# VectorE's order at attention's end, and map loads on SyncE, in a fused attention and mixture-of-experts kernel

## The chip, the cores and the metric

The kernel runs on one core of a Trainium2 chip. The metric is the device time of one execution in microseconds (us). TensorE (PE) does the multiplications and, as PEld, loads their weights; VectorE (DVE) and ScalarE (ACT) work on tiles; GpSimd (POOL) issues gathers, scatters and small transfers; SyncE (SP) issues the large loads.

## The reference

```
scores = scale * q @ k^T ; scores = cap * tanh(scores / cap)      # B=8, H=12, S=448, D=64
attn   = exp(scores - max) / (sum + 1e-9) ; x = attn @ v          # x: 3584 tokens x 768
logits = x @ w_gate + modality_bias[modality] ; e = argmax        # 8 experts
gate   = softmax(logits)[e]
out    = gate * (relu(x @ w1[e]) @ w2[e])                         # w1: 768x1024, w2: 1024x768
```

Every token goes to one expert, so the second half gathers the tokens of one expert and multiplies them with that expert's weights.

## The kernel before, in words

**Attention.** A quad is four heads of one batch; there are NQ = 24, numbered 0 to 23, three per batch. The loop at L748 runs over 25 rounds `i` of three parts `r`. Each part lists its work in order (`ORDER` L714; `LAST` L726 for the round after the last quad). `group` makes scores, tanh and exp; `pv` and `pvs` multiply with v into two PSUM accumulators; `xs` copies an accumulator to SBUF; `tot1`, `tot2` (L590 to L600) add the three key blocks of a half quad on VectorE; `sums` (L606) multiplies with the gate's weights and sums up the denominators on TensorE; `gl` copies that from PSUM; `lt` turns it by transposition; `den` (L638) takes reciprocals and scales the logits (7 small VectorE instructions); `rows` (L662) turns x by blocks of 32 on VectorE and stores it to the DRAM table `xd` by GpSimd. The route of a batch (L227) finds each token's expert and its rank there, and scatters a map of tokens to DRAM (`mapd`).

**Early rows.** The expert with the most tokens is known before the last batches are done. Its first 384 rows are gathered (L788) while attention still runs, and its w1 is loaded and split ahead. Three steps make the first multiplication's input of them. `scale` (L680) multiplies the gathered rows with the reciprocal denominators: twelve VectorE instructions, six for each half of the 768 columns, over both halves at once. `turn_rows(half, banks)` (L992) transposes nine 128x128 blocks on TensorE into three PSUM banks. `split_x` (L1045) makes of each bank a rounded copy (ScalarE, L1048) and a remainder (VectorE, L1050), because every product is a sum of three: high by high, high by low, low by high. The six banks are three tiles of two banks each, so that the third bank of the first half and the first of the second half belong to one tile; the last bank is also where `lt` of quad 22 goes, which `den` of quad 22 reads. `hi_part` and `lo_part` (L690, L694) split w1 in halves of a chunk, on ScalarE and VectorE.

**Slots.** A slot is 384 rows of one expert. `run_slot` (L1112) does `ffn1` (L1052; eight passes `f` of 18 multiplications) and `ffn2` (L1083; 144 multiplications, cut into six stretches `2*t + half` of eight places `f`). Around them stand the next slot's loads and splits. In the first slot the routing of the last batch, the counts and the plan of slots (`slots`, L331) stand between the passes of `ffn1`; the next slot's rows are then gathered, scaled and turned at places of `ffn2` that the table at L1129 to L1134 names. In later slots the rows are turned on VectorE instead (`prepare`, L1030). `ahead` (L1234) issues for slot i its gather, then `rows` (L860: reads the slot's first row into a register, then loads the map, five small transfers for a slot of 384 rows) and `index` (L888, GpSimd) for slot i + 1, then `expert` (L857: SyncE reads the expert's number into a register). The w1 and w2 loads of all slots go through SyncE in program order (L98), into four buffers `raw`.

**Order.** Instructions wrapped in `pin` keep their place behind the instruction written before them on their engine; the others may be placed by the program's scheduler. Around the change nearly all are pinned.

Of the kernel before, what the change touches and what calls it, by code (L numbers as in the profile page):

```python
# [61 lines left out]
TW = W // 128  # L62
RB = -(-NT // W)
RG = RB * W
NOROW = E * RG
KC, FC = DM // 128, FF // 128
# [3 lines left out]
FIXED = 7  # L70
# [14 lines left out]
class Program:  # L85
# [365 lines left out]
    def attention(self, first, rp):  # L451
        tc, nc = self.tc, self.nc
        pe, pin = nc.tensor, self.pin
        with ExitStack() as st:
# [143 lines left out]
            def tot2(q, t):  # L598
                tot = quads[q]["tot"][t]
                pin(nc.vector.tensor_tensor(tot, tot, quads[q]["pt"][t, 2], op=ALU.add))  # L600
# [79 lines left out]
            def scale(q):  # L680
                three = pp.tile([128, KU, 2, S], F32, name="pt", bufs=3).rearrange("p n j s -> p (n j s)")
                banks.extend(tile[:, j] for tile in (score_tile(), score_tile(), score_tile()) for j in range(2))
                self.scale_rows(early[1], [three[:, i * 384 : (i + 1) * 384] for i in range(2 * TW)])

            def part(n):
                k, cs = n if n < KC else (n + 4) % KC, slice(n // KC * 512, n // KC * 512 + 512)
# [15 lines left out]
            def load_parts(*ns):  # L702
# [23 lines left out]
            LAST = (  # L726
                ((pvs, -1), (xs, -1, 0)),
                ((pv, -1, 1, 0), (pv, -1, 1, 1), (pv, -1, 1, 2), (xs, -1, 1)),
                ((sums, -1), (gl, -1), (rows, -1, 0), (rows, -1, 1)),
            )  # L730
            PICK, KNOWN = 2, 6
            PARTS = [PICK * NH + u for u in (6, 7, 9, 10, 12, 13, 15, 16)]
# [3 lines left out]
                *((NQ - 1, r) for r in (0, 0, 1, 1, 1)),  # L736
                *((b * NH + 5 + u, r) for b in range(B - 2) for u, r in ((0, 0), (0, 2), (0, 2), (0, 2), (1, 1), (1, 2))),
            ]
            lgs, pays, routing, raws, banks = {}, {}, [], [], []
            fetch(0, 0)  # L740
            fetch(0, 1)
            begin()
# [5 lines left out]
            for i in range(NQ + 1):  # L748
                for r in (1, 0, 2) if i == 0 else range(3):
                    if (i, r) == (0, 1):  # L750
                        split_hi(0, 1)
                        split_lo(0, 1)
                    if (i, r) == (NQ, 0):
                        tot1(NQ - 1, 1)
                        tot2(NQ - 1, 1)
                    ops = list((ORDER if i < NQ else LAST)[r])
                    if (i, r) == (NQ - 1, 2):
                        ops[-4:] = (scale, 0), (lt, -1), ops[-2]
                    if (i, r) == (NQ - 1, 1):
                        ops.insert(ops.index((sums, -1)), (lambda q: next(routing[0]), 0))  # L760
                    for op, n, *how in ops:
                        q = i + n
                        if 0 <= q and quads[min(q, NQ)]["live"]:
                            op(q, *how)
                    if r == 1:
                        fetch(i + 2, 0)
                    if r == 2:
                        fetch(i + 2, 1)
                        fetch_v(i + 2)
                    for _ in range(STEPS.count((i, r))):  # L770
                        next(routing[0], None)
                    if (i, r) in WAYS:
                        way(WAYS[i, r])
                    if (i, r) == (0, 2):
                        room = self.lp.tile([128, C * 256], F32, name="room", tag="late", bufs=3)[:CP]
                        self.gate_bias(room[:, : B * C * E].rearrange("p (n e) -> p n e", e=E), room[:, B * C * E : B * C * (E + 1)])
                    if (i, r) == (0, 0):
                        pin(nc.vector.memset(self.xg, 0.0))
                    if r == 1 and 1 <= i <= 4:
                        self.empty_map(5 * (i - 1), 5 * i)  # L780
                    if (i, r) == (PICK * NH + 4, 1):
                        chosen = self.early_expert(self.cpool, self.ps_r)
                        next(chosen)
                        meta = next(chosen)
                        e = self.expert(meta, 0)
                    if (i, r) == (KNOWN * NH + 4, 0):
                        early = e, self.rows(meta, 0)[0]
                        self.gather_rows(early[1], known=KNOWN * S)  # L788
                    if (i, r) == (KNOWN * NH + 4, 1):
                        self.early_full(self.ps_r)  # L790
                    if r == 1 and i in PARTS:
                        hi_part(PARTS.index(i))
                    if r == 1 and i + 1 in PARTS:
                        load_parts(PARTS.index(i + 1))
                    if (i, r) == (NQ - 1, 2):
                        self.make_x()
                        for n in range(KEPT, 2 * KC, 2):
                            load_parts(n, n + 1)
                    if (i, r) == (NQ, 0):
                        self.turn_rows(0, banks[:3])  # L800
                        self.split_x(range(3), banks[:3], pin=pin)
                        den(NQ - 2)
                    if (i, r) == (NQ, 1):
                        self.turn_rows(1, banks[3:])
                        self.split_x(range(3, KC), banks[3:], pin=pin)
                        rows(NQ - 2, 0)
                        rows(NQ - 2, 1)
                        hi_part(KEPT)
                        hi_part(KEPT + 1)
                        lo_part(KEPT)  # L810
                    if (i, r) == (NQ, 2):
                        hi_part(KEPT + 2)
                        lo_part(KEPT + 1)
                        hi_part(KEPT + 3)
                        lo_part(KEPT + 2)
                        lo_part(KEPT + 3)
# [40 lines left out]
    def expert(self, meta, row):  # L857
        return self.register(self.nc.sync, meta[row : row + 1, 0:1], E - 1, self.last_sp)

    def rows(self, meta, row, blocks=None):  # L860

        nc = self.nc
        r = self.register(nc.gpsimd, meta[row : row + 1, 1:2], NOROW)
        mt = self.lp.tile([128, TW, MR], F32, name="mt", bufs=6)
        src = self.mapd[ds(r, W)]
        if blocks is None:
            self.pin(nc.gpsimd.dma_start(mt.rearrange("p t w -> p (t w)"), src.rearrange("(p t) w -> p (t w)", t=TW)))
            return mt, None, None
        raw = self.lp.tile([128, 4 * TW, MR], F32, name="map", bufs=2)
        for t, n in blocks:  # L870
            rows = src[t * 128 : (t + n) * 128]
            for a in range(4):
                if n:
                    part = rows.rearrange("(p x) w -> p (x w)", p=32)
                    at = raw[a * 32 : (a + 1) * 32, 4 * t : 4 * (t + n)].rearrange("p x w -> p (x w)")
                else:
                    part = src[:128].rearrange("(g p) w -> p g w", g=4)
                    at = raw[a * 32 : (a + 1) * 32, :4]
                self.pin(nc.gpsimd.dma_start(at, part))
            if n:  # L880
                part = rows.rearrange("(p g t) w -> g p (t w)", p=32, g=4)
                at = mt[:, t : t + n].rearrange("p t w -> p (t w)")
            else:
                part, at = src[:128], mt[:, 0]
            self.pin(nc.gpsimd.dma_start(at, part))
        return mt, raw, blocks

    def index(self, raw, blocks, name="at"):  # L888
# [79 lines left out]
            raw = raws[k] if k < len(raws) else self.load_raw(e, self.w2, k, DM)  # L968
            self.split_w(raw, self.w2s[k], pin=bool(raws))

    def scale_rows(self, mt, homes):

        for i, xn in enumerate(homes):
            half, t = divmod(i, TW)
            for j in range(2):
                rec = mt[:, t, 2 + j * KC + half * 3 : 2 + j * KC + half * 3 + 3]
                self.pin(self.nc.vector.tensor_tensor(
                    xn.rearrange("p (k j d x) -> p j k d x", k=3, j=2, d=2)[:, j],
                    self.xg[:, 4 * t + 2 * j : 4 * t + 2 * j + 2, half * 96 : (half + 1) * 96].rearrange(
                        "p d (k x) -> p k d x", k=3  # L980
                    ),
                    rec.unsqueeze(2).unsqueeze(3).to_broadcast([128, 3, 2, 32]),
                    op=ALU.mult,
                ))
        self.scaled = homes
# [126 lines left out]
    def run_slot(self, cur, n, ahead=None, between=()):  # L1112
# [14 lines left out]
        if nxt and nxt[2]:  # L1127
            if between:
                at = {  # L1129
                    place: lambda k=k: self.load_w1(nxt[0], (k,))  # L1130
                    for k, place in enumerate(((0, 2), (0, 6), (1, 2), (1, 6), (2, 2), (2, 7)))
                }
                at[2, 4] = lambda: self.scale_rows(nxt[1], self.homes())
                at[3, 4], at[4, 2] = lambda: self.transpose_rows(0), lambda: self.transpose_rows(1)  # L1134
            else:
                at = self.prepare(nxt[0], nxt[2], 2 * n)
        elif nxt:
# [91 lines left out]
    def run_slots(self, cur, order):  # L1229
# [4 lines left out]
        def ahead(i, n=TW):  # L1234
# [6 lines left out]
            else:  # L1241
                self.gather(indices[i], 4 * n or 1)
            for s in [i + 1] if i < FIXED else range(i + 1, FIXED + 3) if i == FIXED else ():
                maps.append(self.rows(meta, s, BLOCKS[s]))
                indices[s] = self.index(*maps[s][1:], name="at" if s <= FIXED else f"at{s}")
            if i == FIXED:
                few.append(self.rows_few(meta, FIXED + 2))
# [246 lines left out]
```

## Time and profile before

| | |
|---|---|
| median of 3 runs | 810.02 us (808.63 to 810.65) |
| the profiled execution, of its own | 808.62 us |
| its span in the profile | 806.9 us |
| PE busy | 792.1 us (98%) |
| DVE / ACT / POOL busy | 555.8 / 513.7 / 307.1 us |
| HBM traffic | 173 GB/s over the span |

The span runs from the first to the last instruction; the 1.7 us between it and the execution's own time lie outside. PE's busy time counts matmuls whose ends are modelled, and pipelined ones overlap, so 98% says that PE has little idle time, not that it runs at its peak. The profile also has the clock that TensorE was granted, as a share of 2.4 GHz: 0.50 is 1.2 GHz.

### The profile page before, as it was taken

The page shows a single profiled execution, that of the slowest core. Times are in us where ns is not written, and L with a number is a line of the kernel's source. Part 1 is how long each engine was busy: PE and PEld are TensorE (multiplying, and loading weights), DVE is VectorE, ACT ScalarE, POOL GpSimd, SP SyncE. Part 2 cuts the span into 40 slices and gives each one's busy share as a digit, 9 for nine tenths or more (in the row PEclk, how much of TensorE's full clock was granted, in tenths as well). Part 3 has the DMA queues.
Part 4 walks back from the last instruction along what each step waited for, and adds up shares of the span by engine and source line. Part 5 has one row for each costly group of instructions (what it writes and reads, how often), then busy time and mean ns, then how long its engine had stood idle before and what let it go on. Part 6 is the DMA issues. An engine that isn't in the chain of part 4 may idle for free. (4 is left out here: it accounts for less than half of the span.)

```text
span 806.9 us, 14580 instructions
## 1 busy us (share of the span) xinstructions
PE 792.1 (98%) x5265; PEld 623.4 (77%) x5265; DVE 555.8 (69%) x1082; ACT 513.7 (64%) x597; POOL 307.1 (38%) x376
## 2 busy tenths in 40 slices
PE   7999999999999998999999999999999999999996
PEld 3444454444454444999999999999999999999995
DVE  7889898999999998967274653747537375356820
ACT  7999999999999996345253452534525354245611
POOL 1121423242324155438655173551745417015201
PEclk9999999999999999999999999999999999999998
DMA  6475564646546543576367373563725627247663
GB/s 212 143 238 186 152 191 126 208 155 188 186 150 198 160 157 128 166 279 208 118 199 238 114 229 117 180 235 113 258 100 171 243 98 241 100 146 264 214 240 132
DMA packets 55945, 144.84 MB, mean 180 GB/s; under 512 B 11567, under 2 KB 19585, under 8 KB 55858
## 3 DMA queue, kind: packets, MB, share of 16 engines
q1 hardware_dynamic: 40960, 109.42, 40.3%
q0 software_dynamic: 14752, 34.33, 13.8%
q8 instruction: 46, 0.75, 0.4%
q14 instruction: 41, 0.34, 0.1%
q10 hardware_dynamic: 146, 0.00, 0.0%
HBM read 114.91 MB, written 24.34 MB: 173 GB/s over the span
## 5 line engine op out<-in xcount | busy, mean ns | idle before, releaser
L1067 PE MATMUL ph<-x,ah 128*128 128x384 f32 (+1 forms) x480 | 156.3, 326 | 0.9 <-issue 0.9
L1068 PE MATMUL ph<-x,ah 128*128 128x384 f32 (+1 forms) x480 | 156.0, 325 | 0.0
L1071 PE MATMUL ph<-x,al 128*128 128x384 f32 (+1 forms) x480 | 156.0, 325 | 0.0
L1101 PE MATMUL py<-bh,hh 128*128 128x384 f32 x448 | 150.3, 336 | 0.0
L1101 PE MATMUL py<-bh,hl 128*128 128x384 f32 x448 | 149.8, 334 | 0.0
L1101 PE MATMUL py<-bl,hh 128*128 128x384 f32 x448 | 146.5, 334 | 0.0
L534 ACT ACTIVATE pt<-sc,isc 128x896 f32<-128x896 f32 x144 | 134.8, 1010 | 5.6 <-PE sc L530 2.5
L936 POOL DMA_INDIRECT xg<-xd,at x93 | 115.0, 1237 | 48.3 <-issue 23.8
L674 POOL DMA_DIRECT2D xd<-xs x96 | 61.1, 644 | 185.0 <-DVE xs L668 179.8
L957 DVE TENSOR_TENSOR bl<-raw,bh 128x768 fp32r<-128x768 f32 x80 | 74.3, 956 | 71.3 <-ACT bh L956 58.7
L1077 ACT ACTIVATE hh<-ph 128x384 fp32r<-128x384 f32 (+1 forms) x80 | 37.6, 470 | 134.0 <-PE ph L1071 129.1
L537 ACT ACTIVATE pt<-pt,cabs 128x2688 f32<-128x2688 f32 x48 | 121.9, 2540 | 0.8
L574 PE MATMUL xT<-pt,va 128*64 128x448 f32 x576 | 118.8, 548 | 0.0
L1078 DVE SCALAR_TENSOR_TENSOR hl<-ph,hh 128x384 fp32r<-128x384 f32 (+1 forms) x80 | 42.1, 528 | 109.8 <-ACT hh L1077 109.7
L1067 PEld LDWEIGHTS ph<-x,ah 128*128 128x128 f32 x480 | 90.1, 188 | 2.6 <-ACT ah L692 1.4
L1107 POOL DMA_INDIRECT out_dram<-ot,mt x28 | 33.9, 1212 | 152.9 <-ACT ot L1106 139.3
L1071 PEld LDWEIGHTS ph<-x,al 128*128 128x128 f32 x480 | 90.1, 188 | 0.0
L1068 PEld LDWEIGHTS ph<-x,ah 128*128 128x128 f32 x480 | 90.1, 188 | 0.0
L1101 PEld LDWEIGHTS py<-bh,hh 128*128 128x128 f32 x448 | 84.1, 188 | 1.1 <-issue 0.7
L1101 PEld LDWEIGHTS py<-bh,hl 128*128 128x128 f32 x448 | 84.1, 188 | 0.0
L1101 PEld LDWEIGHTS py<-bl,hh 128*128 128x128 f32 x448 | 83.8, 188 | 0.0
L956 ACT CAST bh<-raw 128x768 fp32r<-128x768 f32 x80 | 64.0, 834 | 26.3 <-DMA raw<-in_w_dram 22.4
(213 smaller groups left out, 1298.1 us busy)
## 6 DMA issues: line engine op xcount, KB each, us to landing
raw<-in_w_dram SPq DMA_DIRECT2D x86, 384.0 KB, 4.1
raw<-in_w_dram SPq DMA_DIRECT2D x60, 512.0 KB, 5.1
kq<-in_kq_dram SPq DMA_DIRECT2D x47, 448.0 KB, 4.4
va<-in_v_dram SPq DMA_DIRECT2D x24, 448.0 KB, 6.2
xd<-xs POOLq DMA_DIRECT2D x96, 112.0 KB, 3.7
cg<-gl SPq DMA_DIRECT2D x22, 224.0 KB, 2.2
raw<-in_w_dram SPq DMA_DIRECT2D x12, 256.0 KB, 4.1
mapd<-pre SPq DMA_DIRECT2D x4, 480.0 KB, 5.6
```

The lines of the kernel that those rows point to most:

```text
L534: pin(nc.scalar.activation(out, sc[:, :, :S], AF.Tanh, scale=self.isc))
L537: pin(nc.scalar.activation(x, x, AF.Exp, scale=self.cabs))
L574: pin(pe.matmul(xT[j * D : (j + 1) * D, :S], va[:, u * D : (u + 1) * D], quads[q]["pt"][t, i][:, j], start=t == i == 0, stop=t == 1 and i ...
L674: (nc.gpsimd.dma_start(self.xd[b * S : (b + 1) * S, a, r * 64 : (r + 1) * 64].rearrange("(n p) f -> p n f", p=32), d["out"][a * 32 : (a + ...
L936: got = self.nc.gpsimd.indirect_dma_start(self.xg[:, c], None, self.xd.rearrange("n a x -> (n a) x"), bass.IndirectOffsetOnAxis(ap=at[:, c ...
L956: a = self.nc.scalar.copy(hi, raw)
L957: b = self.nc.vector.tensor_tensor(lo, raw, hi, op=ALU.subtract)
L1067: nc.tensor.matmul(ph[:, :w], hi[:, fs], self.x[k][:, 0, :w], start=first, stop=False)
L1068: nc.tensor.matmul(ph[:, :w], hi[:, fs], self.x[k][:, 1, :w], start=False, stop=False)
L1071: nc.tensor.matmul(ph[:, :w], lo[:, fs], self.x[k][:, 0, :w], start=False, stop=last)
L1078: nc.vector.scalar_tensor_tensor(hl[:, f, :w], acc, 0.0, hh[:, f, :w], op0=ALU.max, op1=ALU.subtract)
L1101: nc.tensor.matmul(py[half][:, :HALF], self.h[a][:, f, rows], self.w2s[f][c][:, cs], start=left[half] == 3 * FC - 1, stop=left[half] == 0,)
```

## The change

Three edits, all of order or place; the arithmetic is the same.

1. At attention's end. `scale` does the first half's six multiplications only; the second half's six come after the additions `tot1`, `tot2` of quad 23's second half. `den` of quad 22 moves up to directly behind its `lt`. The second half's turn and its `split_x` (`second`) move behind `sums` of quad 23. `hi_part` of two w1 parts moves ahead of it; `rows` of quad 22 and the `lo_part`s come after `rows` of quad 23.
2. In the first slot's `ffn2`, the turns of the next rows move from places (3, 4) and (4, 2) to (3, 6) and (4, 3).
3. `rows` for slots 2 to 7 (counted from 0, the third and later ones of the list `maps`; `0 < i < FIXED`, six calls) reads its register on SyncE and issues its map loads there, behind the last load that SyncE had.

```
             def scale(q):
                 three = ...
-                self.scale_rows(early[1], [three[:, i * 384 : (i + 1) * 384] for i in range(2 * TW)])
+                homes.extend(three[:, i * 384 : (i + 1) * 384] for i in range(2 * TW))
+                self.scale_rows(early[1], homes, (0,))
+
+            def second(q):
+                self.turn_rows(1, banks[3:])
+                self.split_x(range(3, KC), banks[3:], pin=pin)
             LAST = (
-                ((sums, -1), (gl, -1), (rows, -1, 0), (rows, -1, 1)),
+                ((sums, -1), (second, -1), (gl, -1), (rows, -1, 0), (rows, -1, 1)),
             )
                     if (i, r) == (NQ, 0):
                         tot1(NQ - 1, 1)
                         tot2(NQ - 1, 1)
+                        self.scale_rows(early[1], homes, (1,))
                     if (i, r) == (NQ - 1, 2):
-                        ops[-4:] = (scale, 0), (lt, -1), ops[-2]
+                        ops[-4:] = (scale, 0), (lt, -1), (den, -1), ops[-2]
                     if (i, r) == (NQ, 0):
                         self.turn_rows(0, banks[:3])
                         self.split_x(range(3), banks[:3], pin=pin)
-                        den(NQ - 2)
                     if (i, r) == (NQ, 1):
-                        self.turn_rows(1, banks[3:])
-                        self.split_x(range(3, KC), banks[3:], pin=pin)
+                        hi_part(KEPT)
+                        hi_part(KEPT + 1)
+                    if (i, r) == (NQ, 2):
                         rows(NQ - 2, 0)
                         rows(NQ - 2, 1)
-                        hi_part(KEPT)
-                        hi_part(KEPT + 1)
                         lo_part(KEPT)
-                    if (i, r) == (NQ, 2):
                         hi_part(KEPT + 2)
-    def rows(self, meta, row, blocks=None):
+    def rows(self, meta, row, blocks=None, sync=False):
-        r = self.register(nc.gpsimd, meta[row : row + 1, 1:2], NOROW)
+        if sync:
+            r = self.register(nc.sync, meta[row : row + 1, 1:2], NOROW, self.last_sp)
+            load = self.load
+        else:
+            r = self.register(nc.gpsimd, meta[row : row + 1, 1:2], NOROW)
+            load = lambda out, in_: self.pin(nc.gpsimd.dma_start(out, in_))
-                self.pin(nc.gpsimd.dma_start(at, part))      # three places, each now:
+                load(at, part)
-    def scale_rows(self, mt, homes):
+    def scale_rows(self, mt, homes, halves=(0, 1)):
         for i, xn in enumerate(homes):
             half, t = divmod(i, TW)
+            if half not in halves:
+                continue
-                at[3, 4], at[4, 2] = lambda: self.transpose_rows(0), lambda: self.transpose_rows(1)
+                at[3, 6], at[4, 3] = lambda: self.transpose_rows(0), lambda: self.transpose_rows(1)
-                maps.append(self.rows(meta, s, BLOCKS[s]))
+                maps.append(self.rows(meta, s, BLOCKS[s], 0 < i < FIXED))
```

## Rows read from the trace of the kernel before

**Rows 1.** One stage by windows: width, busy us of each engine (instructions), clock, DMA, GB/s
```profile
375.00:722.00 347.00, 347.00 (x2003) 347.00 (x2003) 187.37 (x257) 150.10 (x235) 157.95 (x173) 1.00 0.53 177
```
**Rows 2.** TensorE's timeline at attention's end: start, us, instruction, idle before it
```profile
302.74 0.58 PE L624 MATMUL glog<-tot,pick 128*32 128x448 f32 x3
...
304.00 0.54 PE L624 MATMUL glog<-sh,pick 128*32 128x448 f32 x1
...
309.53 0.65 PE L610 MATMUL sc<-ident,gl 128*112 128x128 f32 x4
...
311.02 1.20 PE L997 MATMUL sc<-ident,pt 128*128 128x128 f32 x9
312.15 2.48 PE L574 MATMUL xT<-pt,va 128*64 128x448 f32 x12
316.31 0.33 PE L997 MATMUL sc<-ident,pt 128*128 128x128 f32 x1 [1.68 <-DVE x L1050]
317.35 1.25 PE L997 MATMUL sc<-ident,pt 128*128 128x128 f32 x8 [0.71 <-DVE lg L653]
...
321.64 0.45 PE L1067 MATMUL ph<-x,ah 128*128 128x384 f32 x1
```
**Rows 3.** VectorE's timeline there
```profile
308.43 3.30 DVE L977 TENSOR_TENSOR pt<-xg,mt 128x192 f32<-128x192 f32 x12
311.64 1.09 DVE L600 TENSOR_TENSOR tot<-tot,pt 128x896 f32<-128x896 f32 x1
...
314.78 1.48 DVE L1050 TENSOR_TENSOR x<-sc,x 128x384 fp32r<-128x384 f32 x3
...
316.94 0.36 DVE L653 TENSOR_TENSOR lg<-sc,pay 112x64 f32<-112x64 f32 x2
...
319.53 1.02 DVE L1050 TENSOR_TENSOR x<-sc,x 128x384 fp32r<-128x384 f32 x2 [0.20 <-ACT x L1048]
```
**Rows 4.** ScalarE's timeline there
```profile
318.26 1.24 ACT L1048 CAST x<-sc 128x384 fp32r<-128x384 f32 x3 [3.05 <-PE sc L997]
```
**Rows 5.** The first slot's matmul line: instruction, count, ns min/median/max, first and last start
```profile
L1067 PEldq EVENT_SEMAPHORE  x1: 51/51/51, 320.6 to 320.6; - x1
```
**Rows 6.** Windows of one us (columns as in rows 1; clock third from the end)
```profile
12.00:13.00 1.00, 0.08 (x2) 0.08 (x2) 0.58 (x2) 0.97 (x2) 0.00 (x0) 1.00 1.03 419
318.00:319.00 1.00, 1.00 (x8) 0.41 (x10) 0.23 (x1) 0.74 (x2) 0.00 (x0) 0.57 0.00 0
321.00:322.00 1.00, 1.00 (x6) 0.36 (x3) 1.00 (x3) 0.58 (x2) 0.07 (x1) 0.72 0.71 163
```
**Rows 7.** Waits of TensorE: waited for, us in total, times, longest
```profile
PE sc L530 <- ACT sh L534: 2.3, 2, 1.5
```
**Rows 8.** VectorE and TensorE where the last batch's ranks are made
```profile
329.21 0.56 DVE L1078 SCALAR_TENSOR_TENSOR hl<-ph,hh 128x384 fp32r<-128x384 f32 x1 [0.99 <-ACT hh L1077]
...
331.22 0.36 DVE L255 TENSOR_TENSOR before<-before,oh 112x8 bf16<-112x8 bf16 x2
...
331.64 0.20 PE L265 MATMUL rank<-before,ones 112*112 112x32 bf16 x1
```
**Rows 9.** TensorE at the first slot's first turn
```profile
362.38 0.82 PE L997 MATMUL xt<-ident,xn 128*128 128x128 f32 x6
363.70 0.55 PE L997 MATMUL xt<-ident,xn 128*128 128x128 f32 x3 [0.50 <-DVE xn L977]
```
**Rows 10.** SyncE's issue (ns min/median/max), landing, timeline; ScalarE's use; GpSimd's wait (times)
```profile
L98 SPq DMA_DIRECT2D raw<-in_w_dram x158: 332/333/1552, 154.2 to 794.5; - x158
...
raw<-in_w_dram SPq DMA_DIRECT2D x60, 512.0 KB, 5.1
...
380.80 2.63 SPq L98 DMA_DIRECT2D raw<-in_w_dram  x3
...
401.07 1.99 ACT L956 CAST ah<-raw 128x1024 fp32r<-128x1024 f32 x2
...
  DMA out_dram<-ot,mt: 13.8, 5
```

More of the change, by code (lines that the diff above doesn't have):

```diff
@@ L738, in attention @@
             ]
-            lgs, pays, routing, raws, banks = {}, {}, [], [], []
+            lgs, pays, routing, raws, banks, homes = {}, {}, [], [], [], []
             fetch(0, 0)
@@ L866, in rows @@
         if blocks is None:
-            self.pin(nc.gpsimd.dma_start(mt.rearrange("p t w -> p (t w)"), src.rearrange("(p t) w -> p (t w)", t=TW)))
+            load(mt.rearrange("p t w -> p (t w)"), src.rearrange("(p t) w -> p (t w)", t=TW))
             return mt, None, None
@@ L884, in rows @@
                 part, at = src[:128], mt[:, 0]
-            self.pin(nc.gpsimd.dma_start(at, part))
+            load(at, part)
         return mt, raw, blocks
```

## The prediction

> **What bounds the kernel now.** I read the windows by stage first, then TensorE's waits and its timeline, because PE is busy nearly throughout. From 375 to 722 us PE has no idle time at all, while VectorE works 187 of 347 us, ScalarE 150 and GpSimd 158 [rows 1]. In these seven slots a faster helper gains nothing; it can only do harm. What the change can gain lies where PE stands. At attention's end it stands 1.68 us before the second turn's first transposition and 0.71 us before its second [rows 2]. The first stop ends 0.05 us after the third remainder of the first half (VectorE, 314.78 + 1.48 = 316.26), though that remainder reads another bank: the two banks are one tile. The second ends 0.05 us after `den` of quad 22 (316.94 + 0.36 = 317.30), which reads the tile's neighbour of the bank that the transposition writes [rows 2, 3]. Then the clock falls: 0.57 as the mean of 318 to 319, 0.72 as that of 321 to 322 [rows 6], so half speed, 1.2 GHz, for 0.86 us of the one and 0.56 of the other, from about 318.14 to 321.56, 3.4 us in which PE did 1.7 us of full-speed work. A third stop, 0.50 us, stands in the first slot's first turn [rows 9]. Together 1.68 + 0.71 + 1.71 + 0.50 = 4.6 us: the most that these parts can give.
>
> **Part 1, attention's end.** Up to 308.43, where `scale` starts, nothing changes. VectorE in the new order: twelve multiplications take 311.64 - 308.43 = 3.21 us to the next start, so six take 1.60 and end at 310.03. `den` of quad 22 needs its `lt`, which ends on PE at 309.53 + 0.65 = 310.18; it takes 1.04 us (316.26 to 317.30), so to 311.3. The three additions take 314.78 - 311.64 = 3.14 (the two between are not shown), so to 314.44; the other six multiplications end at 316.04; the first half's three remainders take 1.48 and end at 317.52 [rows 2, 3].
>
> PE: the last `pv` ends at 312.15 + 2.48 = 314.63, with the additions done 0.1 us before. `sums` runs there at once. For quad 22 it took 302.74 to 304.54, 1.80 us at full clock, so it ends at 316.43. Then comes the second turn, and its first bank is still a neighbour of the third remainder's. That remainder now comes 1.26 us later than before (317.52 for 316.26), because six multiplications stand ahead of it and `den` no longer behind it. PE starts the turn at 317.57, after 1.14 us idle, and takes 1.20 for its nine transpositions, by the first turn at 311.02 [rows 2], to 318.77.
>
> Now nothing covers what follows. Before, `sums` lay behind the second turn, and beside it ScalarE copied and VectorE subtracted the second half's three banks, ending at 319.53 + 1.02 = 320.55 [rows 3, 4]. The first slot's first multiplication has an extra wait in PE's queue that passed at 320.6, with that end [rows 5]. I take it that the multiplications' banks lie on the six banks of the turns, so that they wait for the last remainder. From the end of the turn (317.35 + 1.25 = 318.60) to that remainder's end were 1.95 us, and from the first copy 2.29; the new last remainder ends at 318.77 + 1.95 = 320.7 to 320.9. I take 320.8. PE stands 318.77 to 320.85, 2.08 us, and `ffn1` starts at 320.85 for 321.64 [rows 2]: 0.79 us earlier. So the two stops of 2.39 us become two of 3.22, and what is won is the half-speed stretch, if it goes.
>
> It should come again. Before, it came after PE had stood 2.39 of 2.72 us with one transposition between; a single stop of at most 1.5 us near 12 us [rows 7] left the clock at 1.00 [rows 6]. Now PE stands 3.22 of 4.42 us, from 316.43 to 320.85, with 1.20 us of transpositions between. If the 3.4 us at half speed lie wholly on `ffn1` they cost 1.71 us, if half of them fall into the idle time 0.85; without a fall, nothing. I take 1.2, nearer the middle of the two: `ffn1` is then where a start at 322.05 would have put it, 0.4 us behind the kernel before.
>
> The Trainium skill, "TensorE: Matmul & The Clock Gate", section "Part 1: The HAM clock gate", says that the clock depends on how busy PE has been of late, not on one gap. By that rule the two stops count together, and the change keeps what lowers the clock; gap by gap, 1.14 us would leave the clock and 2.08 is a size that the trace does not show. Without a fall the sum is that of rival B.
>
> There is a floor as well. The rank matmuls stand behind the third pass of `ffn1`, at 331.61 to 331.64, and VectorE's `before` was ready at 331.22 + 0.36 = 331.58: no room [rows 8]. VectorE has the same work up to there in the new order. Of its idle time only the 0.99 us before the second `hl` can go [rows 8], and the last remainder is 0.25 us later (320.8 for 320.55). So `before` can come at most 0.74 us earlier, and PE with it; of the 0.79 us won without a fall 0.74 stay. With the fall the chain has room and PE loses nothing there. The `hi_part`s and `lo_part`s are moved inside idle ScalarE time and behind the remainders; their halves of w1 serve from the fifth pass on, some 12 us later, so nothing.
>
> **Part 2, the turns in `ffn2`.** Two places later are six multiplications of 347.0 / 2003 = 0.173 us [rows 1], 1.04 us. The turn's last three transpositions waited 0.50 us for data [rows 9]; 1.04 us later the data are there 0.54 us ahead, unless PE has won more than that on the gathers. With the fall both chains are late alike; without it both are 0.74 early. So 0.50 us are won. The second turn shows no wait; it moves by three multiplications, 0.52 us, towards the next slot's first one, which could cost 0 to 0.5 us there; I take 0, the copies behind it being short.
>
> **Part 3, the maps on SyncE.** Six calls put a register read, like the one that `expert` makes there already, and five transfers (ten in the last) into SyncE's queue, between the last w2 load of a slot and the first w1 load of the next. A transfer's issue costs 0.33 us at the median and 1.55 at the most [rows 10], so 2 to 8 us a slot (3 to 16 in the last). Behind them wait the w1 loads: the first four were out by 383.43, and ScalarE took up the first at 401.07, without a wait; a load takes 5.1 us to land [rows 10]. That leaves some 12 us of room, which hides all but the slow end of the last call. GpSimd is relieved of these issues, in a stage where it is idle 189 of 347 us [rows 1]. I take 0, from the median, which 158 issues stand for; less than nothing is excluded, as PE has no idle time there.
>
> **The sum.** +0.4 - 0.5 + 0 = -0.1 us against the profiled execution's own 808.62 (its span of 806.9 and 1.7 outside it). That execution is the fastest of those shown; the median of the runs is 810.02, 1.4 more. I put the sum to the median: 809.9. Its own range, by the cost of the fall (0 to 0.5 more, or 0.35 less) and by 1 us to either side for how the runs scatter: 808.5 to 811.4.
>
> **The rivals.** B, the clock stays up: `ffn1` 0.74 us early by the floor, and 0.50: 1.24 us faster, 808.8. For it: a stop at 12 us without a fall, and transpositions between the new stops. Against it: more idle time than where it fell. C, SyncE's queue becomes the bound: slower. Before, GpSimd's map transfers waited 13.8 us in five times for an output to leave the buffer that they write [rows 10]. Such a wait on SyncE, added to issues at 1.55 us, would hold w1 loads beyond that room; PE then stands in each of six slots. At 0.5 to 1 us a slot that is 3 to 6 us: about 814. It decides only if one of these waits is over 4 us and all issues are slow; in the new place the buffer's last reader is slots back. D, the first slot's data come later than PE (VectorE's end of the plan shifted by the scheduler): the 0.50 us stay lost, 810.4. E, the last remainder does not hold `ffn1`, and VectorE's chain finds idle time that I do not see: up to the 4.6 us above, 805.4 to 807.5. Against it stands the floor.
>
> **How the numbers follow.** Forecast 0.62, B 0.19, C 0.06, D 0.07, E 0.06. About 0.3%, 2.4 us, is what a measurement of this kernel can tell from no change: E alone is faster by more, C alone slower by more. Faster 0.06, same 0.88, slower 0.06. The range takes in B and D and a scatter of 1.2 us: 807.6 to 811.4.
>
> **What would show it.** Right: `sums` before the second turn at 314.6; a stop of about 1.1 us before that turn, ended by the third remainder; one of about 2.1 us before the first multiplication of `ffn1`, ended by the last; clock 0.50 once more between 319 and 325; no stop at the first slot's turn; SyncE's map issues at 0.3 to 0.5 us, and 375 to 722 without idle PE. Wrong: `ffn1` starting with the turn's end, a rank matmul that waits on `before` while the clock was low, or ScalarE's w1 copies waiting on loads.

## The result and the profile after

The changed kernel is slower: 817.25 us at the median (815.74 to 818.71, six runs) against 810.34 for the kernel before on the same chip (808.31 to 812.87, six runs), a ratio of 1.0071 with a 95% interval of 1.0050 to 1.0092. The prediction was 809.9, in a range of 807.6 to 811.4. A change of -0.1 us was forecast; measured are +6.9 us by the medians and +5.75 (4.1 to 7.5) by the ratio. The profiled execution took 815.92 us, its span 814.3.

TensorE's timeline at attention's end came out nearly as forecast [rows 2]:

```profile
312.31 2.48 PE L574 MATMUL xT<-pt,va 128*64 128x448 f32 x12
314.72 0.56 PE L624 MATMUL glog<-tot,pick 128*32 128x448 f32 x1
...
317.69 1.20 PE L1007 MATMUL sc<-ident,pt 128*128 128x128 f32 x9 [1.26 <-DVE x L1060]
321.15 0.52 PE L1077 MATMUL ph<-x,ah 128*128 128x384 f32 x1 [2.26 <-DVE x L1060]
...
332.63 0.20 PE L265 MATMUL rank<-before,ones 112*112 112x32 bf16 x1
```

`sums` runs at 314.7, the second turn waits for the third remainder, `ffn1` for the last one. The rank matmul comes 0.99 us later than before [rows 8]; 0.16 of it stood already at the last `pv` (312.31 for 312.15), ahead of all that part 1 moves on PE, so 0.83 are part 1's. The windows there (width, PE busy, clock third from the end) show why [rows 6]:

```profile
319.00:321.00 2.00, 0.00 (x0) 1.00 0.01 4
321.00:322.00 1.00, 0.85 (x3) 0.65 0.00 0
322.00:323.00 1.00, 1.00 (x4) 0.50 0.07 16
...
324.00:325.00 1.00, 1.00 (x5) 0.64 0.74 115
```

The clock falls as `ffn1` begins, and all of the half-speed stretch lies on `ffn1`. From 375 to 722 us PE again has no idle time [rows 1]:

```profile
375.00:722.00 347.00, 347.00 (x2003) 347.00 (x2003) 187.69 (x257) 150.29 (x235) 138.13 (x143) 1.00 0.53 177
```

So SyncE's queue became no bound. Of its 35 map transfers, 28 took 0.32 us each to issue and seven 0.62, about 1.9 us for a call of five (ns, min/median/max):

```profile
L98 SPq DMA_DIRECT2D map<-mapd x28: 3/316/795, 377.8 to 632.9; - x28
L98 SPq DMA_DIRECT2D mt<-mapd x7: 605/622/754, 379.8 to 633.5; - x7
```

The loss is at the end of the program. GpSimd's timeline has the last gather of the branch's first batch, and the last scatter, of the kernel before and then of the changed one:

```profile
738.29 1.05 POOL L936 DMA_INDIRECT xg<-xd,at  x1 [0.30 <-issue]
...
800.82 0.97 POOL L1223 DMA_INDIRECT out_dram<-of,index  x1 [0.33 <-POOLq L1262]
```

```profile
740.17 1.73 POOL L944 DMA_INDIRECT xg<-xd,at  x1 [0.53 <-issue]
...
802.70 0.97 POOL L1233 DMA_INDIRECT out_dram<-of,index  x1 [1.05 <-POOLq L1272]
```

The last scatter is 1.88 us later, but the span is 7.4 us longer. What lies behind it shows only where the last line of the program is asked for (ns, min/median/max, first and last start). DRAIN and INC_SWDGE_SEM are the profile's names of instructions that the kernel's text does not have. Before:

```profile
L1489 POOLq INC_SWDGE_SEM  x7: 228/254/302, 726.8 to 732.6; - x7
L1489 POOLq DRAIN  x3: 46/109/2186, 803.9 to 806.6; - x3
```

After:

```profile
L1499 POOLq INC_SWDGE_SEM  x7: 1142/1178/1216, 726.9 to 738.2; - x7
L1499 POOLq DRAIN  x3: 46/109/8241, 805.2 to 814.0; - x3
```

GpSimd's first DRAIN of the end section takes 8.24 us for 2.19: 6.05 of the 7.4 us. The other engines stand at the end and wait for it; SyncE's last wait is 6.0 us for 2.0. A transfer still under way is not what DRAIN waits for: it runs from 805.25 to 813.49, and for 807 to 814 the window (width, POOL busy, clock, DMA, GB/s) shows no DMA at all:

```profile
807.00:814.00 7.00, 0.00 (x0) 0.50 0.00 0
```

Seven INC_SWDGE_SEM, which the build puts between the gathers at the branch, take 1.18 us for 0.25, and the last gather of that batch comes 1.9 us later. The busy times and the chain on the page hold none of this: these instructions are not counted as busy, and the chain begins at the last scatter. The Trainium skill, "VectorE: DVE Perf Modes", section "The DRAIN you can't avoid", gives the DRAINs that frame a program a constant 12 ns or so on all five engines. Here GpSimd's goes from 46 ns to 8.24 us, and the measurement decides.

### The profile page after: what moved, and what is told of

The parts are those of the page before. It is cut to its first block, busy times and chain, and to the rows that moved or that the text cites. A ratio compares the mean times of both kernels' runs of the same rounds, so it can differ in the third digit from the quotient of the medians.

```text
span 814.3 us, 14593 instructions
## 1 busy us (share of the span) xinstructions
PE 792.3 (97%) x5265; PEld 624.5 (77%) x5265; DVE 556.0 (68%) x1082; ACT 513.9 (63%) x597; POOL 283.7 (35%) x341
## 5 line engine op out<-in xcount | busy, mean ns | idle before, releaser
L1117 POOL DMA_INDIRECT out_dram<-ot,mt x28 | 30.9, 1103 | 188.1 <-ACT ot L1116 167.1
```

## Experiments

Ratios are to the kernel before in the same runs, with their 95% intervals.

| | edit | GpSimd's transfers | INC_SWDGE_SEM, median ns | DRAIN ns | ratio |
|---|---|---|---|---|---|
| before | | 312 | 254 | 2186 | 1 |
| after | parts 1 to 3 | 277 | 1178 | 8241 | 1.0071 (1.0050 to 1.0092) |
| 1 | parts 1 and 2 | 312 | 254 | 2191 | 1.0011 (1.0001 to 1.0020) |
| 2 | part 3 | 277 | 1178 | 8241 | 1.0081 (1.0064 to 1.0098) |
| 3 | after, 10 back | 287 | 1304 | 9037 | 1.0132 (1.0115 to 1.0149) |
| 4 | after, 15 back | 292 | 1360 | 9443 | 1.0115 (1.0097 to 1.0132) |
| 5 | before + 40 | 352 | 599 | 4475 | 1.0097 (1.0073 to 1.0121) |
| 6 | before + 100 | 412 | 1342 | 9378 | 1.0143 (1.0121 to 1.0165) |
| 7 | after + 24 | 301 | 1402 | 9697 | 1.0175 (1.0153 to 1.0197) |
| 8 | part 2 | 312 | 254 | 2186 | 0.9994 (0.9981 to 1.0008) |
| 9 | 1, filled | 312 | 254 | 2187 | 0.9982 (0.9965 to 0.9998) |
| 10 | after + 48 | 325 | 1617 | 1362 | 1.0079 (1.0052 to 1.0106) |
| 11 | part 1 | 312 | 254 | 2187 | 1.0014 (0.9997 to 1.0031) |
| 12 | part 2, filled | 312 | 254 | 2187 | 0.9997 (0.9980 to 1.0014) |
| 13 | after + 72 | 349 | 368 | 2910 | 1.0042 (1.0024 to 1.0061) |
| 14 | 13, filled | 349 | 368 | 2910 | 1.0031 (1.0007 to 1.0054) |

**1 and 2: the parts apart.** The first undoes part 3 in the changed kernel, the second is part 3 alone:

```
-                maps.append(self.rows(meta, s, BLOCKS[s], 0 < i < FIXED))
+                maps.append(self.rows(meta, s, BLOCKS[s]))
```

> The changed kernel with all maps of slots three to seven (and the eighth's) issued by GpSimd again, so parts 1 and 2 alone. The traces of the two kernels differ most after the last scatter: GpSimd's DRAIN in the end section takes 8.24 us for 2.19, and its seven INC_SWDGE_SEM at the branch 1.18 us each for 0.25, while GpSimd issued 277 transfers for 312. Theory T (the end costs by how many transfers GpSimd's queue has issued since some earlier point, and falls to little when a bound is passed, which lies between the two counts): 312 transfers again, so DRAIN near 2.2 us and INC_SWDGE_SEM near 0.25; what is left is attention's end and the first slot's turn, about +0.5 us: 810.5 to 811.5 us. Theory E (the longer end comes from VectorE's new order or from where the instructions now lie): DRAIN stays near 8 us, 816.

> The kernel before with the maps on SyncE alone, part 3 without parts 1 and 2. Theory T: 277 transfers from GpSimd, so DRAIN near 8.2 us and INC_SWDGE_SEM near 1.18: 6 us or somewhat more over the kernel before, 815 to 817 us. Theory E: DRAIN near 2.2 us, and the time that of the kernel before, 810. If SyncE's queue itself were the loss (rival C of the prediction), PE would show idle time between 375 and 722 us and the end would be as before.

Parts 1 and 2 cost 0.9 us (0.1 to 1.6) and leave DRAIN as it was; part 3 alone costs 6.5 us (5.2 to 7.9) and has the DRAIN of the changed kernel to the nanosecond:

```profile
L1494 POOLq INC_SWDGE_SEM  x7: 1142/1178/1216, 726.1 to 737.3; - x7
L1494 POOLq DRAIN  x3: 46/109/8241, 804.1 to 812.9; - x3
```

Its last scatter is issued at 801.08, 0.26 us later than before; 0.26 + 6.05 is 6.3 us, against 6.2 between the two profiled executions. So DRAIN is nearly all that part 3 costs. PE is busy for all of 375 to 722 us there too: rival C of the prediction is out, and so is theory E.

**3 and 4: some of the map transfers back on GpSimd.**

```
-                maps.append(self.rows(meta, s, BLOCKS[s], 0 < i < FIXED))
+                maps.append(self.rows(meta, s, BLOCKS[s], 0 < i < FIXED - 1))   # in 4: FIXED - 2
```

> The changed kernel, with only the ten map transfers of the last call (slot index 7) issued by GpSimd again: 287 transfers in all, 273 up to the branch for 263 and 298. Theory T: the INC_SWDGE_SEM rose by 0.07 us over six transfers in the one trace and by 0.07 over four in the other, which puts the point where they fall near 280 transfers; DRAIN then comes after it and is short, under 1 us, while INC_SWDGE_SEM still takes 1.2 to 1.3 us: 809 to 811 us. A rival T2 (the more of the work SyncE takes, the longer the end, in proportion): 25 of 35 transfers moved, so DRAIN 2.2 + 25/35 x 6.05 = 6.5 us and INC_SWDGE_SEM 0.9: about 815. Theory E: near 8 us, 816.

> The changed kernel, with the map transfers of slot indices 6 and 7 issued by GpSimd again: 292 transfers in all, 278 up to the branch. Theory T: DRAIN about 0.5 to 1.2 us, INC_SWDGE_SEM either 1.3 us or already near 0.1: 809 to 811 us. Rival T2: DRAIN 2.2 + 20/35 x 6.05 = 5.7 us, INC_SWDGE_SEM 0.8: about 814.

DRAIN did not fall, as theory T had it, nor follow the share moved, as T2 had it. It rose, by 0.080 us for each transfer that came back: 9.04 and 9.44 us. The times are 3.2 and 1.9 us over what experiments 1 and 2 add up to in the same runs (1.0092), about 2 us to either side, where DRAIN accounts for 0.8 and 1.2.

**5, 6 and 7: more transfers on GpSimd's queue, nothing moved.** To the kernel before (40, 100) and to the changed one (24) small transfers are added, spread over the slots, into a tile that nothing reads:

```
+        extra, pad = [], self.lp.tile([128, 32], F32, name="pad", bufs=1)
...
+            if i in (2, 3, 4, 5, 6):       # in 7, 10, 13 and 14: (1, 2, 3, 4, 5, 6)
+                for _ in range(8):         # 20 in the second; 4, 8, 12, 12 in 7, 10, 13, 14
+                    j = len(extra)
+                    extra.append(j)
+                    self.pin(nc.gpsimd.dma_start(pad[j % 4 * 32 : j % 4 * 32 + 32, j // 4 : j // 4 + 1], self.mapd[0:32, 0:1]))
```

> The kernel before, with 40 more transfers on GpSimd's queue (eight in each of five slots, 32 values each into a tile that nothing reads): 352 in all, 338 up to the branch. Nothing is moved to SyncE, and VectorE's order is the old one. So far DRAIN was 8.24 us at 277 transfers, 9.04 at 287, 9.44 at 292 (0.080 us a transfer) and 2.19 at 312, which on the same slope is 0.080 x (n - 284.7). Theory T (a count of GpSimd's transfers that starts again at some point): DRAIN 0.080 x 67 = 5.4 us, INC_SWDGE_SEM 0.25 + 40 x 0.013 = 0.75, the time 3 to 3.5 us over the kernel before. Rival M (what counts is that the maps come from SyncE): DRAIN 2.2, no more than 0.5 us slower. Rival W (GpSimd's work in the slots delays the gathers): PE idle between 375 and 722 us.

> The same with 100 more transfers, 20 in each of five slots: 412 in all. Theory T: the two lines of DRAIN against the count start at 174 and at 285, 110 transfers apart, and the first was still rising at 292 and had fallen by 298 or so; the second then falls between 403 and 409, and at 412 DRAIN is 0.080 x (412 - 395) = 1.4 us, less than with no extra transfer: 0.8 us faster than the kernel before by this, less what GpSimd's 50 us of extra issues cost elsewhere. If a count without a fall is behind it: 0.080 x 127 = 10.2 us and 8 us slower. Rival M: DRAIN 2.2 us and the time that of before.

> The changed kernel with 24 extra transfers on GpSimd's queue, four in each of six slots: 301 in all, the maps still on SyncE. Theory T: DRAIN 0.080 x (301 - 284.7) = 1.3 us for 8.24, so 6.9 us faster than the changed kernel, although it does more: within 1 us of the kernel before, 809 to 810. Rival M: DRAIN stays at 8.2 us or grows to 10.2, 816 to 818.

Rival M is out: with every map on GpSimd, 40 and 100 extra transfers make DRAIN 4.5 and 9.4 us.

But a plain count with one slope is out as well: 301 transfers gave 9.70 us and 412 gave 9.38, where 1.3 and 1.4 had been expected. In experiments 3 to 7 every DRAIN that theory T drew from its lines missed. What fits is an account that grows as GpSimd issues and is cleared at some point, to which different transfers add differently; that is an inference from the DRAINs, no trace shows the account. In the order of the counts the DRAINs rise from 8.24 us (277 transfers) to 9.70 (301), are low at 312 and 325 (2.19, 1.36) and rise again to 9.38 (412): one fall, between 301 and 312.

The added lines cost something that has nothing to do with this queue. In all six kernels that have them (5, 6, 7, 10, 13, 14) a multiplication of `ffn1` in the slots takes 338 to 339 ns on average, in the other ten kernels 336. Before and experiment 5, 375 to 722 us (busy us, mean ns, idle before):

```profile
L1068 PE MATMUL ph<-x,ah 128*128 128x384 f32 x336 | 112.9, 336 | 0.0
```

```profile
L1068 PE MATMUL ph<-x,ah 128*128 128x384 f32 x336 | 113.8, 339 | 0.0
```

Three such lines of 336 make 1008 multiplications, and PE is 2.9 us later behind them, with no idle time shown. It is the same for 4 transfers a slot and for 20, so it comes with the added tile or code and not with the number of transfers; how, no run shows. In 5 the time rose by 7.8 us (5.9 to 9.8): 2.3 are DRAIN, 2.9 these multiplications, and 2.6 stay open.

**8: part 2 alone.**

```
-                at[3, 4], at[4, 2] = lambda: self.transpose_rows(0), lambda: self.transpose_rows(1)
+                at[3, 6], at[4, 3] = lambda: self.transpose_rows(0), lambda: self.transpose_rows(1)
```

> The kernel before with the two turns of a slot's rows two and one places later in ffn2, part 2 alone; GpSimd issues 312 transfers. By the prediction the stop of 0.50 us before the last transpositions of the first slot's turn goes, and nothing else moves: 0.5 us faster. A rival: the second turn now comes too near to the next slot's first multiplication, PE shows a stop there in each slot (0.1 to 0.5 us in seven), and the time is the same or up to 3 us slower.

The stop before the turn [rows 9] is gone, and the 0.5 us are what was expected, though the interval includes none. That stop varies from one profile to the next: with the old places it was 0.3 to 1.1 us in five profiles (before, 2, 5, 6, 11); with the new ones it is gone in nine, and was 0.2 and 1.1 us in two (1, 4).

**9 and 12: PE kept busy in its stops.** The ninth adds to the first experiment matmuls of ones around the second turn; the twelfth adds seven before that turn in the old order.

```
             def second(q):
+                self.warm(self.ps_r, 5)
                 self.turn_rows(1, banks[3:])
+                self.warm(self.ps_r, 10)
```

> Parts 1 and 2 with all maps on GpSimd (as in the first experiment) and, in PE's two stops at attention's end, matmuls of ones into a bank that nothing reads: five before the second turn (0.22 us each by the four at 10.43 in the trace of before, so 1.1 us for a stop of 1.26) and ten behind it (2.2 for 2.26). In the first experiment the clock fell in these stops and 6.8 us at half speed followed, in the changed kernel 3.4. If the idle time is what lowers it, it stays at 1.00 and the first slot's first matmul runs at full speed from the same start: 1.7 to 3.4 us faster than the first experiment, which was 0.9 over before: 0.8 to 2.0 us faster than the kernel before (rival B of the prediction, with VectorE's floor, said 1.24). If not, as the first experiment, +0.9.

> The kernel before with part 2 and seven matmuls of ones before the second turn, 1.5 us for its stop of 1.68; the stop of 0.71 inside the turn stays. If the idle time before the second turn lowers the clock in the kernel before, it stays at 1.00 now: ffn1 starts near 320.9 as it did in the one run of the old order without a fall (second experiment), behind the last remainder, and the rank matmuls wait for VectorE: 0.7 us faster by the prediction's floor, and 0.5 by the turns: 0.5 to 1.2 us faster than the kernel before. If the fall comes from elsewhere: as part 2 alone, -0.5 to 0.

Windows of experiment 1 and then of 9:

```profile
315.00:320.00 5.00, 2.51 (x25) 0.99 0.27 82
320.00:325.00 5.00, 3.97 (x12) 0.50 0.17 30
```

```profile
315.00:320.00 5.00, 4.92 (x36) 1.00 0.33 86
320.00:325.00 5.00, 4.90 (x29) 1.00 0.15 23
```

The turn and `ffn1` start when they did, the clock stays at full speed there, and by the ratios the kernel is 2.3 us faster than experiment 1 (0.9982 for 1.0011, in other runs on another chip) and 1.5 us (0.2 to 2.8) faster than the kernel before. The second interval only just leaves out none, and the medians differ by 0.6 us: likely faster than both, by little. The Trainium skill, "TensorE: Matmul & The Clock Gate", section "Part 1: The HAM clock gate", has the clock follow how busy PE has been of late; this pair agrees. In the old order the filling gained nothing that can be measured (-0.2 us, -1.6 to 1.1); there the clock falls only at times, as the profiles listed under experiment 11 show.

**10, 13 and 14: the account cleared late.** 48, 72 and 72 extra transfers in the changed kernel; in 14 also the matmuls of experiment 9.

> The changed kernel with 48 extra transfers on GpSimd's queue, eight in each of six slots: 325 in all. A plain count of transfers is refuted: 301 with 24 extra ones gave DRAIN 9.70 us, where 312 with the maps gives 2.19. What is left of theory T: an account grows by about 0.08 us of DRAIN with each transfer and is cleared when it is full, and transfers of different sizes fill it differently; a map call's five fill more than five of the small ones. The highest DRAIN so far is 9.70. Theory T: with 48 the account is cleared before the end and DRAIN is 1.5 to 3.5 us: 5 to 6.5 us faster than the changed kernel, with 48 transfers more. Rival M (maps on SyncE make the end long whatever else is queued): DRAIN 8.2 us or, growing by 0.06 for each, 11.1; 820 us or more.

> The changed kernel with 72 extra transfers on GpSimd's queue, twelve in each of six slots: 349 in all, maps on SyncE. With 48 the account was cleared inside the branch, between the sixth and the seventh INC_SWDGE_SEM (1.67 us, then 0.20), with 3.2 us in which GpSimd's queue shows nothing, and PE then stood 3.4 us for the last gathers. 24 transfers more should move the clearing ahead of the branch, into a slot where GpSimd has idle time. Theory T: all INC_SWDGE_SEM 0.3 to 0.6 us, DRAIN 1.36 + 24 x 0.06 = 2.8 us, no stop of 3.4 us, and the time falls to that of parts 1 and 2 alone plus 0.6 to 1.5 us: 5 us faster than the changed kernel, 1 to 2.5 over the kernel before. If the maps on SyncE cost something beside the end (rival C), 4 us or more over the kernel before stay.

> The same with the matmuls of ones in PE's stops at attention's end (five and ten, as in the ninth experiment): all three parts of the change, with both costs found so far taken away. Theory: the clock stays at 1.00 from 316 to 330 us, DRAIN 2.8 us; 1.7 to 2.5 us faster than the run without them, so from 1 us over the kernel before to 1 us under it. If the clock's fall was not what parts 1 and 2 lost, as without them.

```profile
L1505 POOLq INC_SWDGE_SEM  x7: 196/1617/1668, 732.4 to 749.3; - x7
L1505 POOLq DRAIN  x3: 46/109/1362, 816.7 to 818.6; - x3
```

With 48 more transfers on GpSimd's queue DRAIN falls from 8.24 to 1.36 us (1.5 to 3.5 were expected): something is cleared, and rival M is out for the changed kernel too. But the time did not fall with it. I take it that the clearing fell into the branch: GpSimd stood 3.43 us before the next gather, six INC_SWDGE_SEM of 1.6 us had slowed those ahead of it, and PE then stood 3.4 us for what is made of them. Behind that stop the clock fell for 6.8 us (width, PE busy, clock third from the end), which the added lines' 2.9 us come on top of.

```profile
745.02 1.00 POOL L944 DMA_INDIRECT xg<-xd,at  x1 [0.30 <-issue]
749.45 1.00 POOL L944 DMA_INDIRECT xg<-xd,at  x1 [3.43 <-issue]
```

```profile
755.00:760.00 5.00, 4.28 (x13) 0.50 0.30 86
```

With 72 there is no such stop, and both kinds are short: INC_SWDGE_SEM of 0.34 to 0.41 us, DRAIN 2.91 (2.8 expected).

The time is 3.4 us over before (2.0 to 5.0), 2.3 under the changed kernel's 5.75, where 5 were expected. Parts 1 and 2 (0.9), DRAIN (0.7) and the added lines (2.9) make 4.5, within the interval, so nothing is left over for the maps on SyncE. In its profiled execution PE has another 2.7 us of stops put down to issue at 381 to 386 us, which no other run had there; whether these are in the median, is open. Experiment 14 took off another 0.9 of the 1.7 to 2.5 expected; by the intervals it could be the whole of that, or none.

**11: part 1 alone** (experiment 1 with the old places of part 2).

> Part 1 alone, VectorE's new order at attention's end on the kernel before: old turns in ffn2, maps on GpSimd. From the prediction's sum +0.4 us; from the two experiments (parts 1 and 2: +0.9; part 2 alone: -0.5) about +1.4. GpSimd's DRAIN 2.19 us. The half-speed stretch, if there is one, lies on ffn1 and costs 1.7 us where the old order hides part of it in idle time and sums.

It costs 1.1 us, with an interval that just includes none. All eight profiles of the new order without filling (after, 1, 3, 4, 7, 10, 11, 13) show half speed after 319 us, for 3.4 us in six and 6.8 in two (1, 10). Of the old order without filling (before, 2, 5, 6, 8), three show it and two, 2 and 5, do not; of the three filled ones none.

The executions without a fall tell what the order itself is worth. Experiment 2 (old order), then 9 (new order, filled):

```profile
312.39 2.48 PE L574 MATMUL xT<-pt,va 128*64 128x448 f32 x12
320.92 0.42 PE L1072 MATMUL ph<-x,ah 128*128 128x384 f32 x1 [0.62 <-DVE x L1055]
330.84 0.20 PE L265 MATMUL rank<-before,ones 112*112 112x32 bf16 x1
```

```profile
312.45 2.48 PE L574 MATMUL xT<-pt,va 128*64 128x448 f32 x12
321.29 0.41 PE L1079 MATMUL ph<-x,ah 128*128 128x384 f32 x1
331.26 0.20 PE L265 MATMUL rank<-before,ones 112*112 112x32 bf16 x1
```

From that `pv` to the rank matmul the old order takes 18.45 us without a fall (18.51 in 5, 18.44 in 12) and 19.4 to 19.5 with one (before, 6, 8); the new order takes 18.81 (18.82 in 14), and 20.1 to 20.3 with a fall of 3.4 us. So in these profiles the new order is later in both cases, by 0.4 us and by 0.6 to 0.9, and what experiment 9 gains is the clock's.

## Why the prediction was wrong

- **What PE does at attention's end** was right: `sums` at 314.63 (314.72), the turn at 317.57 behind the third remainder (317.69), `ffn1` at 320.85 behind the last (321.15), in an execution that is 0.16 us late ahead of it.
- **The clock's fall** was rightly expected, but mis-sized: I took 1.2 us, between 0.85 and 1.71. It was the upper end, since nothing of it lay in idle time. The rank matmul came 0.83 us later for 0.4 (0.99 with the 0.16 from ahead of it). In the old order, moreover, the fall is not there in each run: without it `ffn1` starts 0.96 us earlier there (8.53 us behind that `pv` in experiment 2, 9.49 before), so the 0.79 us that I put down to the new order are what the fall had cost ahead of `ffn1` in the one profile. The remark that a stop near 12 us left the clock up was one execution's too: in experiments 1, 2, 3 and 14 the clock fell there for 3.4 us. The floor held: 0.74 us forecast, 0.68 and 0.67 in the new order without a fall (9, 14). Parts 1 and 2 together: -0.1 forecast, +0.9 measured.
- **Part 2** was right in place and size, as far as 0.5 us can be told.
- **Part 3** is the step that failed: "I take 0". Alone it cost 6.5 us (5.2 to 7.9), 6.05 of them in GpSimd's DRAIN behind the last scatter. On the side I looked at it held: issues of 0.32 and 0.62 us, no idle PE, so rival C's mechanism was wrong even where its 814 came nearer. On GpSimd's side I wrote that it "is relieved of these issues" in a stage where it is idle. I counted what the moved transfers cost the queue that receives them, and not what they leave behind in the queue that they are taken from. With 35 transfers fewer on it, its DRAIN at the end of the program took 6 us more; that an account was cleared elsewhere is what fits the other runs, and not shown.
- **The sum** took what lies outside the changed stages as unchanged, and the range left no room for it. The trace of before held a hint that I did not read: a DRAIN of 2.19 us at the end, and INC_SWDGE_SEM that rise from 0.23 to 0.30 us between the second and the last of the seven.

## What to carry to other kernels

When transfers leave GpSimd's queue or are added to it, compare its DRAIN at the end and its INC_SWDGE_SEM at a branch before and after; DRAIN moved by up to 8 us here (1.36 to 9.70), and no busy time counts it. Read the stretch from the last counted instruction to the end of the span as a stage of its own. Where a change moves idle time of PE next to dense work, price the clock's fall on that work in full, or fill the stop with matmuls that nobody reads; and look at several profiles of the kernel before, since a fall that is there only at times is no fixed sum to be won. A probe has costs of its own: compare the lines that it should not touch.

## What the runs showed of the hardware

- GpSimd's DRAIN at the end took from 1.36 to 9.70 us in sixteen kernels, the same to 5 ns in kernels with the same transfers on its queue (2186 to 2191 ns in six, 8241 in two). INC_SWDGE_SEM goes along: 0.25, 0.60, 1.18, 1.34 us beside DRAINs of 2.19, 4.48, 8.24, 9.38. From 277 to 292 transfers each added 0.080 us; of the small ones 24 added 0.061 each (7), 60 added 0.082 each (5 to 6), and 48 led to a fall (10), where INC_SWDGE_SEM took 1.62 us beside a DRAIN of 1.36.
- What the account holds, and what clears it, no run shows. The Trainium skill, "DMA: Bandwidth & Descriptors", section "SWDGE vs HWDGE vs iDMA", says that GpSimd writes the descriptors of its transfers in software, into rings in SBUF. An account of entries in a ring, gone through when it is full or must be empty, would fit; I found no one ring size that gives all the DRAINs, so it stays a guess.
- In some executions (9, 11, 13 and 14) PE has three or more short stops put down to issue, of 0.2 to 0.9 us within 5 us, once at 381 us (13) and else at 734 to 742, behind the branch. In 9 and 11 the clock then fell for 3.4 us (at 737 and 741). What the stops are is open.
